# Sliding-window attention and a two-layer MLP on one core: both layers in turn, attention pairs evenly apart, and the third batch loaded ahead of the second weights

## The chip, the core and the metric

The kernel runs on one core of a Trainium2 chip. A core has TensorE (PE in the profile) for matmuls, VectorE (DVE), ScalarE (ACT) and GpSimd (POOL) for element work, and SyncE (SP), which here only issues DMAs. GpSimd and ScalarE can issue DMAs as well. TensorE writes to PSUM, which has eight banks of 128 x 512 float32 values; everything else is in SBUF. The metric is the device time of one execution in microseconds (us): before the change a median of 378.02, from 376.28 to 382.29 in three runs. The execution that the profile shows spans 374.9 us.

## The reference

Attention with a causal window of 64 keys over 8 batches, 8 heads, 576 positions and a head size of 64; then two matrix products with `h - tanh(h)` between them, over 4608 tokens.

```python
# q, k, v: (8, 8, 576, 64)
scores = (1 / np.sqrt(64)) * np.matmul(q, k.transpose(0, 1, 3, 2))
rel = pos[:, None] - pos[None, :]
scores = np.where((rel >= 0) & (rel < 64), scores, -1e9)
attn = np.exp(scores - scores.max(-1, keepdims=True))
attn = attn / (attn.sum(-1, keepdims=True) + 1e-9)
x = np.matmul(attn, v).transpose(0, 2, 1, 3).reshape(4608, 512)
h = x @ w_in                 # (4608, 2048)
out = (h - np.tanh(h)) @ w_out   # (4608, 512), float32
```

## The kernel before

**Attention** is worked by pairs of heads: a batch has four pairs, and pair g belongs to batch g // 4. Each pair goes through these steps. Loads of q and k (`load`, `load_all`) and of v (`load_v`, `load_v_all`) come on GpSimd's DMA queue and turn float32 into bf16. `cast` (L112) brings two heads side by side. `tr` (L259) transposes q and k on TensorE into a PSUM bank, and ScalarE and VectorE copy them to `qT` and `kT`; for batch 7 `bounce` (L124) and `tr_dma` (L136) do it through DRAM with a transposing DMA on SyncE. `scores` (L326) makes nine matmuls in three groups, each followed by an exponential on ScalarE into `PT`. `masking` (L334) multiplies by the window's mask on VectorE. `pv` (L342) makes nine matmuls of `PT` with the value windows `vw` into banks 5 to 7, and `norm` (L349) divides on VectorE into `xs`. Once two pairs or a whole batch are done, x is transposed into a chunk tile `xT`: by `x_tr` (L359) on TensorE or by `x_dma` (L371) on SyncE. Batches 0 and 1 use the variants `tr_heads`, `tr_rows`, `tile_scores` and `tile_pv`, in the same sense.

A **value window** is 128 keys: window j holds block j-1 in partitions 0 to 63 and block j in partitions 64 to 127. `cast_v` (L170) fills `vb` from the loaded v. `windows_v` (L157) then copies a whole window from `vb` by DMA. The other way is `keys_v` (L174), which copies the upper half only, and `shift_v` (L179), which fills the lower halves from the upper ones: on VectorE (`shift_dve`, L465) or by one DMA. There is one `vb`, two `vw` (even and odd batches), one buffer for a loaded v and two each for q and k.

**The MLP** is worked by chunks of 512 tokens, nine in all. A first-layer op h(c, m) is four 128 x 512 matmuls (L403) into a bank, tanh on ScalarE (L408), and a subtraction on VectorE into `gT` (L415), which frees the bank. `hp_bank` names the bank: two in turn, or three in some stretches. A second-layer op y(c, st) is four matmuls (L429) of a quarter of the sum; after four of them ScalarE copies the bank (L434) and SyncE sends 256 KB to the output (L436).

**The order is written by hand.** The program is a row of slots h = 0, 1, 2, ... `OPS` (L438) puts at most one op into a slot, and `items` (filled by `at`, L451) any number of attention steps or loads. The loop at L622 records each slot's op, its items, and then the subtraction of a first-layer op. Every engine works its own instructions in that order, so a slot is a position in each engine's queue and no fixed time. `AHEAD` (L387) says how many second-layer ops of the chunk before run ahead of a chunk's first layer. With a lead of n, a chunk has n second-layer ops in a row, then both layers in turn, then n first-layer ops in a row. `FIRST` (L422) reorders the first eight second-layer ops so that those that need only the first half of `w_out` come first.

`STEPS` (L572) gives for batches 2 to 7 the slot a of each pair: transposes at a and a+2, scores at a+5, a+7, a+9, masking at a+11, `pv` at a+13 to a+15, norm at a+15. `LOADS` gives the slots of the loads of k, q and v, and `VALUES` the first slot and the step of the v casts and the first slot of the windows. `pace` (L460) holds a load on GpSimd until a given first-layer op is done.

Of the kernel before, what the change touches and what calls it, by code (L numbers as in the profile page):

```python
# [15 lines left out]
def kernel(  # L16
# [9 lines left out]
    nc = tc.nc  # L26
    B, H, S, D = q.shape
    NP = H // 2
    NJ = S // 64
# [7 lines left out]
    NC = NT // TOK  # L37
    M = d_ff // 128
# [32 lines left out]
    vw = [const.tile([128, NJ, H, D + 1], BF16, name=f"vw{i}") for i in range(2)]  # L71
# [3 lines left out]
    qT = [const.tile([128, 2, S], BF16, name=f"qt{i}") for i in range(NR)]  # L75
# [6 lines left out]
    def move(eng, o, i):  # L82
        if eng is nc.scalar:
            nc.scalar.activation(o, i, ACT.Copy)  # L84
        else:
            eng.tensor_copy(o, i)  # L86
# [83 lines left out]
    def cast_v(b, pr, eng=nc.gpsimd):  # L170
        move(eng, vb[:, :, 2 * pr:2 * pr + 2, 0:D].rearrange("p e h d -> p h e d"),
             stage.pop((b, pr, "v")).rearrange("p h (e d) -> p h e d", d=D))

    def keys_v(b, j, eng=nc.sync):  # L174

        eng.dma_start(out=vw[b % 2][64:128, j].rearrange("p h c -> p (h c)"),
                      in_=vb[8 * j:8 * j + 8].rearrange("p e h c -> p e (h c)"))
# [15 lines left out]
    def w_in_tile(ki, m):  # L193
        i = m // 8
        f = 512 * (m // 4 % 2) + m % 4
        return w_in_sb[i][:, ki, f:f + 4 * 127 + 1:4]
# [41 lines left out]
    def chunk_tile(c):  # L238
        if c not in xT:
            xT[c] = xt_pool.tile([128, WPC, 2, 128], BF16, tag="xT", name="xT")  # L240
        return xT[c]
# [142 lines left out]
    gT = {}  # L384
    HID = {}

    AHEAD = {1: 8, 2: 8, 3: 6, 4: 4, 5: 4}  # L387

    def hp_bank(c, m):

        m0 = M - AHEAD.get(c, 0)
        if m < m0:
            return m % 2
        a, b = m0 % 2, 1 - m0 % 2
        return {8: (a, b, 2), 6: (a, 2, b), 4: (a, b, 2)}[M - m0][(m - m0) % 3]

    def hp_mm(c, ms, split):

        outs = [ps[:, hp_bank(c, m), :] for m in ms]
        for kis in ((0, 2), (1, 3)) if split else ((0, 1, 2, 3),):  # L400
            for m, hp in zip(ms, outs):
                for ki in kis:
                    nc.tensor.matmul(hp, w_in_tile(ki, m),  # L403
                                     chunk_tile(c)[:, :, ki % 2, 64 * (ki // 2):64 * (ki // 2) + 64],
                                     start=(ki == 0), stop=(ki == 3))
        for m, hp in zip(ms, outs):
            th = sm_pool.tile([128, TOK], F32, tag="th", name="th")
            nc.scalar.activation(th, hp, ACT.Tanh)  # L408
            HID[c, m] = hp, th

    def g_sub(c, m):
        hp, th = HID.pop((c, m))
        if m == 0:
            gT[c] = g_pool.tile([128, M, TOK], BF16, tag="gT", name="gT")
        nc.vector.tensor_tensor(gT[c][:, m, :], hp, th, ALU.subtract)  # L415

    def yp_bank(c, s):
        if c == 0:
            return (2, 1, 2, 2)[s]
        return (0, 2)[s % 2] if c == NC - 1 else 2  # L420

    FIRST = (0, 1, 4, 5, 2, 3, 6, 7)  # L422

    def yp_mm(c, st):
        s, part = divmod(st, 4)
        yp = ps[:, yp_bank(c, s), :]
        for i in range(4):
            m = 4 * part + i
            nc.tensor.matmul(yp, gT[c][:, m, s * 128:(s + 1) * 128], w_out_sb[:, m, :],  # L429
                             start=(m == 0), stop=(m == M - 1))  # L430
# [7 lines left out]
    OPS = {}  # L438
    for m in range(M):
        OPS[2 * m] = "h", 0, m  # L440
        OPS[32 * NC + 2 * m + 1] = "y", NC - 1, m
    for c in range(1, NC):
        n = AHEAD.get(c, 0)
        for m in range(M):
            OPS[32 * c + (n + 2 * m if m < M - n else 16 + m)] = "h", c, m
            st = FIRST[m] if c == 1 and m < 8 else m
            OPS[32 * c + (m if m < n else 2 * m - n + 1)] = "y", c - 1, st

    items = {}

    def at(h, fn, *args):  # L451
        items.setdefault(h, []).append((fn, args))
# [3 lines left out]
    def flush():  # L456
        if done:
            y_out(*done.pop())
# [10 lines left out]
    V, A, G, Y = nc.vector, nc.scalar, nc.gpsimd, nc.sync  # L469
# [63 lines left out]
        cast(g, "k", eng)  # L533
        cast(g, "q", eng)

    at(8, lambda: nc.vector.memset(vw[1][0:64, 0], 0.0))
    at(9, cast_pair, 4, V)
    at(11, cast_pair, 5, V)
    at(12, lambda: [cast_v(1, pr, V) for pr in range(NP)])
    at(13, lambda: [keys_v(1, j, (G, Y)[j % 2]) for j in range(NJ)])  # L540
    at(13, load_w_out, 0)
    at(13, load_w_out, 1)
    at(13, load_v_all, 2)
    for g in 8, 9, 10, 11:
        at(13, load, g, "k", G)
        at(13, load, g, "q", G)
    at(19, cast_pair, 6, V)
    at(22, cast_pair, 7, V)
    for g, t, s0, s1 in (4, 11, 13, 14), (5, 14, 15, 15), (6, 21, 24, 25), (7, 24, 27, 28):
        at(t, tr_rows, g, "k", 2, V)  # L550
        at(t + 1, tr_rows, g, "q", 3, A)
        at(s0, tile_scores, g, 0, (4, 5))
        at(s1, tile_scores, g, 1, (6, 7) if g < 6 else (4, 5))
    at(25, shift_dve, 1, 0, 4)
    for pr in range(NP):
        at(27 + 2 * pr, tile_pv, 4 + pr, (6, 7))
    at(31, x_tr, 1, 0, 0, 4, 3, A)
    at(32, x_tr, 1, 0, 4, 9, 4, A)
    at(36, x_tr, 1, 1, 0, 4, 3, V)
    at(37, x_tr, 1, 1, 4, 9, 4, A)  # L560
    at(33, lambda: nc.vector.memset(qT[1], 0.0))

    at(100, more_zeros, 0)
    at(118, more_zeros, 1)

    def behind_x(b):

        last = ((b + 1) * NJ - 1)
        nc.gpsimd.tensor_copy(tick, chunk_tile(last // WPC)[0:1, last % WPC, 0, 0:1])

    LOADS = {3: (50, 50, 50), 4: (73, 75, 77), 5: (98, 100, 102), 6: (130, 134, 126), 7: (145, 143, 162)}
    STEPS = {2: (39, 44, 49, 54), 3: (63, 73, 79, 84), 4: (93, 102, 108, 114), 5: (121, 127, 133, 138),  # L572
             6: (146, 153, 160, 167), 7: (174, 182, 190, 198)}
    VALUES = {2: (38, 0, 42), 3: (61, 1, 65), 4: (87, 1, 91), 5: (112, 2, 120), 6: (140, 2, 152), 7: (170, 2, 178)}
    at(36, cast_pair, 8, G)
    at(37, cast_pair, 9, G)
    at(40, cast_pair, 10, G)
    at(45, cast_pair, 11, G)
    for g in range(2 * NP, B * NP):
        b, pr = divmod(g, NP)  # L580
        a = STEPS[b][pr]
        cv, cs, ky = VALUES[b]
        at(cv + cs * pr, cast_v, b, pr, V if b == 2 else G)
        if b == 7:
            at(a - 14, cast_q, g)
            at(a - 13, cast, g, "k")
            at(a - 12, bounce, g, "q")
            at(a - 11, bounce, g, "k")
            at(a - 6, tr_dma, g, "q")
            at(a - 5, tr_dma, g, "k")  # L590
        else:
            if b > 2:
                at(a - 7, cast, g, "q")
                at(a - 5, cast, g, "k")
            at(a, tr, g, "q", 3, A, V)
            at(a + 2, tr, g, "k", 3, A)
        for i in range(3):
            at(a + 5 + 2 * i, scores, g, i, 4)
            at(a + 13 + i, pv, g, i)
        at(a + 11, masking, g)  # L600
        at(a + 15, norm, g)
        if b < 5:
            if pr % 2:
                at(a + 16, x_tr, b, pr // 2, 0, 4, 3, V)
                at(a + 17, x_tr, b, pr // 2, 4, 9, 3, A)
        elif pr == NP - 1:
            at(a + 16, x_dma, b)
        if pr == 0:
            for j in range(NJ):
                at(ky + j // 2, windows_v, b, j, Y)  # L610
            if b == 2:
                continue
            hk, hq, hv = LOADS[b]
            for h, f in sorted(((hq, (load_all, b, "q")), (hk, (load_all, b, "k")), (hv, (load_v_all, b))),
                               key=lambda x: x[0]):
                if b > 3:
                    at(h, pace, h)
                if (b, h) == (7, hv):
                    at(h, behind_x, 5)
                at(h, *f)  # L620

    for h in range(32 * NC + 32):  # L622
        op = OPS.get(h)
        if op:
            flush()
        if op and op[0] == "h":
            c, m = op[1:]
            if c == 0 and m == 0:
                hp_mm(c, (0, 1), True)
            elif c > 0 or m > 1:  # L630
                hp_mm(c, (m,), False)
        elif op:
            yp_mm(*op[1:])
            if op[2] % 4 == 3:
                done.append((op[1], op[2] // 4))
        for fn, args in items.pop(h, []):
            fn(*args)
        if op and op[0] == "h":
            g_sub(*op[1:])
# [31 lines left out]
```

The softmax here doesn't subtract the row's maximum and nothing guards it: scores larger than these inputs give would overflow.

## Time and profile before

| What | From the profile before |
|---|---|
| Span of the profiled execution | 374.9 us |
| TensorE, VectorE, ScalarE, GpSimd busy | 327.1, 201.2, 183.9, 104.5 us |
| First-layer matmuls (L403), second-layer (L429) | 150.2, 142.6 us busy |
| One subtraction (L415), one tanh (L408) | 690, 598 ns |
| Half a norm's product (L357), one masking (L336) | 755, 747 ns |
| First-layer ops begin, last tanh begins | 25.6, 356.25 us |
| Halves of `w_out` landed | 52.2, 57.7 us |
| v, k, q of batch 2 landed | 61.4 to 67.7 us |

Busy time of TensorE includes the overlap of matmuls in its pipeline, so the table of lines gives more per matmul than the pace at which they follow each other. The page cuts the span into 40 slices of 9.4 us and gives each engine's busy share in tenths; the clock row is the TensorE clock as a share of full speed. In the waits, a line names who waited, for whom, the total, the number of waits and the longest. In the chain, each piece is the work or the transfer that the next piece waited for.

### The profile page before, as it was taken

What the parts mean: (1) busy time and instruction counts of PE and PEld (TensorE: products, weight loads), DVE (VectorE), ACT (ScalarE), POOL (GpSimd) and SP (SyncE); (2) the same over time, 40 slices, a digit from 0 to 9 for tenths busy, and PEclk for the clock granted to TensorE, in tenths of its full rate; (3) what the DMA queues carried; (4) which work ended last, traced back from release to release, by engine and by line L of the source; (5) the groups of instructions that cost most, each with busy time, mean ns of one, the idle gap of its engine ahead of it and who ended that gap; (6) DMA issues with size and microseconds to landing.
All of it is one profiled execution on the core that took longest, in us unless ns stands there. A gap on an engine that the chain in (4) does not pass through costs nothing.

```text
span 374.9 us, 6143 instructions
## 1 busy us (share of the span) xinstructions
PE 327.1 (87%) x2366; PEld 178.8 (48%) x2398; DVE 201.2 (54%) x332; ACT 183.9 (49%) x338; POOL 104.5 (28%) x153
## 2 busy tenths in 40 slices
PE   7776889988889988999899937797799999999995
PEld 3543454555445544555565513453355544444442
DVE  4557684448556764567668613565466543433400
ACT  3534663766456745667565713554254444444321
POOL 8911804507024616631337325110000000000000
PEclk9989999999999999999999996999699999999999
DMA  8999899792639279345956983448941311001012
GB/s 158 168 174 185 134 200 182 133 221 57 118 69 180 59 120 175 73 78 101 154 93 92 186 149 81 79 104 165 175 96 40 60 60 58 28 28 59 28 57 84
DMA packets 49918, 41.80 MB, mean 111 GB/s; under 512 B 18496, under 2 KB 43584, under 8 KB 49888
## 3 DMA queue, kind: packets, MB, share of 16 engines
q0 software_dynamic: 20816, 18.73, 33.9%
q1 hardware_dynamic: 28720, 22.24, 25.7%
q10 hardware_dynamic: 352, 0.43, 0.4%
q8 instruction: 19, 0.31, 0.3%
q14 instruction: 11, 0.09, 0.1%
HBM read 36.70 MB, written 11.21 MB: 128 GB/s over the span
## 4 chain that ended last, share of the span: by engine, by line
PE 57%; DMA 14%; DVE 12%; ACT 5%; issue 5%; POOL 4%; SPq 2%; ACTq 0%; POOLq 0%; DVEq 0%
PE ps L429 24%; PE ps L403 24%; DMA vall<-in_v_dram 7%; DMA vw<-vb 6%; DVE xs L357 5%; DVE gT L415 3%; PE ps L346 2%; PE ps L330 2%; ACT th L408 2%; PE ps L263 2%; SPq L161 1%; PE ps L363 1%; DVE qt L86 1%; DMA qt<-qd 1%; ACT ysb L434 1%
## 5 line engine op out<-in xcount | busy, mean ns | idle before, releaser
L403 PE MATMUL ps<-xT,wi 128*128 128x512 bf16 x576 | 150.2, 386 | 4.8 <-DVE gT L415 4.1
L429 PE MATMUL ps<-w_out_sb,gT 128*128 128x512 bf16 x545 | 142.6, 383 | 3.8 <-ACT ysb L434 1.3
L415 DVE TENSOR_TENSOR gT<-ps,th 128x512 bf16<-128x512 f32 x144 | 98.6, 690 | 86.3 <-ACT th L408 85.2
L408 ACT ACTIVATE th<-ps 128x512 f32<-128x512 f32 x144 | 86.0, 598 | 89.2 <-PE ps L403 85.6
L403 PEld LDWEIGHTS <-wi 128*128 128x128 bf16 x576 | 61.2, 114 | 53.6 <-issue 11.4
L429 PEld LDWEIGHTS <-gT 128*128 128x128 bf16 x576 | 54.0, 98 | 63.1 <-issue 11.6
L332 ACT ACTIVATE pt<-ps 128x384 bf16<-128x384 f32 x72 | 35.2, 489 | 47.7 <-PE ps L330 47.7
L346 PE MATMUL ps<-vw,pt 128*128 128x130 bf16 x216 | 25.7, 221 | 16.2 <-DMA vw<-vb 13.5
L357 DVE TENSOR_TENSOR xs<-ps,rc 64x576 bf16<-64x576 f32 x48 | 36.2, 755 | 1.1
L434 ACT ACTIVATE ysb<-ps 128x512 f32<-128x512 f32 x36 | 21.4, 595 | 17.3 <-PE ps L429 17.1
L346 PEld LDWEIGHTS <-pt 128*128 128x128 bf16 x216 | 18.2, 98 | 23.8 <-issue 4.2
L86 DVE COPY qt<-ps 64x576 bf16<-64x576 bf16 x20 | 15.2, 759 | 22.5 <-ACT qt L84 22.5
L330 PE MATMUL ps<-qt,kt 128*128 128x128 bf16 x216 | 24.2, 222 | 1.9 <-DMA qt<-qd 1.8
L86 POOL COPY kb<-kall 96x768 bf16<-96x768 bf16 x24 | 19.9, 829 | 17.5 <-DMA kd<-kb 10.1
L86 POOL COPY vb<-vall 72x1024 bf16<-72x1024 bf16 x20 | 20.6, 1052 | 13.8 <-DMA vall<-in_v_dram 13.8
L330 PEld LDWEIGHTS <-kt 128*128 128x128 bf16 x216 | 16.7, 99 | 13.1 <-issue 3.4
L86 POOL COPY qb<-qall 96x768 bf16<-96x768 bf16 x20 | 16.7, 834 | 17.1 <-DMA qall<-in_q_dram 8.6
L353 DVE RECIPROCAL rc<-ps 128x9 f32<-128x9 f32 x24 | 5.2, 218 | 27.0 <-PE ps L346 26.7
L336 DVE TENSOR_TENSOR pt<-pt,ps 128x1152 bf16<-128x1152 bf16 x24 | 17.9, 747 | 1.0 <-ACT pt L332 1.0
L463 POOL COPY tick<-gT 1x1 bf16<-1x1 bf16 x12 | 2.1, 179 | 49.3 <-DVE gT L415 49.3
L84 ACT ACTIVATE xT<-ps 128x512 bf16<-128x512 bf16 (+4 forms) x20 | 8.6, 479 | 14.5 <-PE ps L363 14.5
L84 ACT ACTIVATE kt<-ps 128x576 bf16<-128x576 bf16 x20 | 13.0, 651 | 4.5 <-PE ps L263 4.5
(74 smaller groups left out, 205.8 us busy)
## 6 DMA issues: line engine op xcount, KB each, us to landing
out_dram<-ysb SPq DMA_DIRECT2D x36, 256.0 KB
vw<-vb SPq DMA_DIRECT2D x48, 130.0 KB
vall<-in_v_dram POOLq DMA_DIRECT2D x7, 576.0 KB, 11.5
qall<-in_q_dram POOLq DMA_DIRECT2D x5, 576.0 KB, 6.3
kall<-in_k_dram POOLq DMA_DIRECT2D x5, 576.0 KB, 6.7
wi<-in_moe_w_in_dram POOLq DMA_DIRECT2D x2, 1024.0 KB, 15.1
w_out_sb<-in_moe_w_out_dram POOLq DMA_DIRECT2D x2, 1024.0 KB, 13.9
kall<-in_k_dram POOLq DMA_DIRECT2D x11, 144.0 KB, 15.4
```

What stands on the lines that cost most here:

```text
L84: nc.scalar.activation(o, i, ACT.Copy)
L86: eng.tensor_copy(o, i)
L330: nc.tensor.matmul(sp[:, i, :], kT[g % NR][:, 64 * j:64 * j + 128], qT[g % NR][:, :, 64 * j:64 * j + 64], start=True, stop=True)
L332: nc.scalar.activation(PT[g % NPT][:, 3 * grp:3 * grp + 3, :], sp, ACT.Exp, scale=scale)
L336: nc.vector.tensor_tensor(p, p, mask.unsqueeze(1).to_broadcast([128, 2 * NJ, 64]), ALU.mult)
L346: nc.tensor.matmul(ps[:, 5 + grp, 130 * i:130 * i + 130], PT[g % NPT][:, j, :], vw[b % 2][:, j, 2 * pr:2 * pr + 2, :], start=True, stop=True)
L357: nc.vector.tensor_tensor(xo[r, :, :, pr, :], ov[r, :, :, h, 0:D], rc[r].to_broadcast([64, 3, 3, 64]), ALU.mult)
L403: nc.tensor.matmul(hp, w_in_tile(ki, m), chunk_tile(c)[:, :, ki % 2, 64 * (ki // 2):64 * (ki // 2) + 64], start=(ki == 0), stop=(ki == 3))
L408: nc.scalar.activation(th, hp, ACT.Tanh)
L415: nc.vector.tensor_tensor(gT[c][:, m, :], hp, th, ALU.subtract)
L429: nc.tensor.matmul(yp, gT[c][:, m, s * 128:(s + 1) * 128], w_out_sb[:, m, :], start=(m == 0), stop=(m == M - 1))
L434: nc.scalar.activation(ysb, ps[:, yp_bank(c, s), :], ACT.Copy)
```

## The change

The change rewrites the hand-written order; what is computed stays the same.

- *The MLP's order.* Chunk 0's and chunk 1's first layers come first; second-layer ops of chunk 0 begin at slot 49. From chunk 2 on the two layers take turns throughout, without a lead, eight slots later than before. `FIRST` goes, and the first six ops of chunk 0 use three banks.
- *The start.* v of batch 1 is cast at slot 6 instead of 12. v, k and q of batch 2 are loaded ahead of `w_out`, which moves from slot 13 to 27 behind the windows of batch 2. Casts of batch 2 go from GpSimd to VectorE, and its windows are built by `keys_v` and shifts on VectorE.
- *The pairs* stand 7 to 8 slots apart (before: 5 to 10). Batch 4's x is transposed by DMA instead of TensorE; the x transposes of batches 2 and 3 have slots of their own (`XTR`).
- *The values* of batches 5 to 7 are cast earlier against their use, and their windows are built by `keys_v` and one shift DMA on SyncE. The load of v for batch 7 no longer waits for batch 5's x.

```diff
-    AHEAD = {1: 8, 2: 8, 3: 6, 4: 4, 5: 4}
-
     def hp_bank(c, m):
-
-        m0 = M - AHEAD.get(c, 0)
-        if m < m0:
-            return m % 2
-        a, b = m0 % 2, 1 - m0 % 2
-        return {8: (a, b, 2), 6: (a, 2, b), 4: (a, b, 2)}[M - m0][(m - m0) % 3]
+        return m % 3 if c == 0 and m < 6 else m % 2
...
-            return (2, 1, 2, 2)[s]
+            return 2
...
-    FIRST = (0, 1, 4, 5, 2, 3, 6, 7)
...
-        OPS[32 * NC + 2 * m + 1] = "y", NC - 1, m
-    for c in range(1, NC):
-        n = AHEAD.get(c, 0)
-        for m in range(M):
-            OPS[32 * c + (n + 2 * m if m < M - n else 16 + m)] = "h", c, m
-            st = FIRST[m] if c == 1 and m < 8 else m
-            OPS[32 * c + (m if m < n else 2 * m - n + 1)] = "y", c - 1, st
+        OPS[32 + 2 * m] = "h", 1, m
+        OPS[49 + 2 * m if m < 8 else 56 + m] = "y", 0, m
+        for c in range(2, NC + 1):
+            if c < NC:
+                OPS[32 * c + 8 + 2 * m] = "h", c, m
+            OPS[32 * c + 9 + 2 * m] = "y", c - 1, m
...
-    at(12, lambda: [cast_v(1, pr, V) for pr in range(NP)])
-    at(13, lambda: [keys_v(1, j, (G, Y)[j % 2]) for j in range(NJ)])
-    at(13, load_w_out, 0)
-    at(13, load_w_out, 1)
-    at(13, load_v_all, 2)
+    at(6, lambda: [cast_v(1, pr, V) for pr in range(NP)])
+    at(7, lambda: [keys_v(1, j, (G, Y)[j % 2]) for j in range(NJ)])
+    at(7, load_v_all, 2)
     for g in 8, 9, 10, 11:
-        at(13, load, g, "k", G)
-        at(13, load, g, "q", G)
+        at(7, load, g, "k", G)
+        at(7, load, g, "q", G)
...
+    at(26, lambda: [cast_v(2, pr, V) for pr in range(NP)])
...
+    at(27, lambda: [keys_v(2, j, G) for j in range(NJ)])
+    at(27, load_w_out, 0)
+    at(27, load_w_out, 1)
+    at(27, load_all, 3, "q")
+    at(27, load_all, 3, "k")
+    at(27, load_v_all, 3)
+    at(41, shift_dve, 2, 0)
+    at(42, shift_dve, 2, 4)
...
-    LOADS = {3: (50, 50, 50), 4: (73, 75, 77), 5: (98, 100, 102), 6: (130, 134, 126), 7: (145, 143, 162)}
-    STEPS = {2: (39, 44, 49, 54), 3: (63, 73, 79, 84), 4: (93, 102, 108, 114), 5: (121, 127, 133, 138),
-             6: (146, 153, 160, 167), 7: (174, 182, 190, 198)}
-    VALUES = {2: (38, 0, 42), 3: (61, 1, 65), 4: (87, 1, 91), 5: (112, 2, 120), 6: (140, 2, 152), 7: (170, 2, 178)}
+    LOADS = {4: (74, 75, 77), 5: (101, 104, 97), 6: (132, 136, 119), 7: (156, 160, 150)}
+    STEPS = {2: (30, 38, 46, 54), 3: (63, 70, 77, 84), 4: (91, 98, 105, 112), 5: (119, 126, 134, 142)}
+    XTR = {9: (58, 60), 11: (70, 71), 13: (88, 90), 15: (100, 102)}
+    VALUES = {3: (64, 1, 68), 4: (84, 1, 90), 5: (107, 2, 115), 6: (124, 5, 142), 7: (156, 5, 174)}
...
-        a = STEPS[b][pr]
+        a = STEPS[b][pr] if b in STEPS else 8 * g - 44
...
-        if b < 5:
-            if pr % 2:
-                at(a + 16, x_tr, b, pr // 2, 0, 4, 3, V)
-                at(a + 17, x_tr, b, pr // 2, 4, 9, 3, A)
-        elif pr == NP - 1:
+        if g in XTR:
+            at(XTR[g][0], x_tr, b, pr // 2, 0, 4, 3, V)
+            at(XTR[g][1], x_tr, b, pr // 2, 4, 9, 3, A)
+        if b > 3 and pr == NP - 1:
             at(a + 16, x_dma, b)
...
-                at(ky + j // 2, windows_v, b, j, Y)
+                at(ky + j // 2, windows_v if b < 5 else keys_v, b, j, Y)
+            if b > 4:
+                at(ky + 7, shift_v, b, 0, NJ - 1)
...
-                if (b, h) == (7, hv):
-                    at(h, behind_x, 5)
```

More of the change, by code (lines that the diff above doesn't have):

```diff
@@ L534, in cast_pair @@
         cast(g, "q", eng)
-    at(8, lambda: nc.vector.memset(vw[1][0:64, 0], 0.0))
+    at(3, lambda: nc.vector.memset(vw[1][0:64, 0], 0.0))
+    at(6, lambda: [cast_v(1, pr, V) for pr in range(NP)])
+    at(7, lambda: [keys_v(1, j, (G, Y)[j % 2]) for j in range(NJ)])
+    at(7, load_v_all, 2)
+    for g in 8, 9, 10, 11:
+        at(7, load, g, "k", G)
+        at(7, load, g, "q", G)
     at(9, cast_pair, 4, V)
     at(11, cast_pair, 5, V)
-    at(12, lambda: [cast_v(1, pr, V) for pr in range(NP)])
@@ L540 @@
-    at(13, lambda: [keys_v(1, j, (G, Y)[j % 2]) for j in range(NJ)])
-    at(13, load_w_out, 0)
-    at(13, load_w_out, 1)
-    at(13, load_v_all, 2)
-    for g in 8, 9, 10, 11:
-        at(13, load, g, "k", G)
-        at(13, load, g, "q", G)
[L547 to L553, printed above, removed]
@@ L554 @@
-    at(25, shift_dve, 1, 0, 4)
-    for pr in range(NP):
[L556 to L561, printed above, removed]
+    at(18, cast_pair, 6, V)
+    at(20, cast_pair, 7, V)
+    at(22, shift_dve, 1, 0, 4)
+    for g, t, ka, qa, a, b in ((4, (11, 12, 13, 14), 6, 7, (4, 5), (6, 7)), (5, (14, 15, 15, 15), 2, 3, (4, 5), (6, 7)),
+                             (6, (19, 20, 21, 22), 2, 3, (4, 5), (4, 5)), (7, (21, 22, 24, 25), 2, 3, (4, 5), (4, 5))):
+        at(t[0], tr_rows, g, "k", ka, V)
+        at(t[1], tr_rows, g, "q", qa, A)
+        at(t[2], tile_scores, g, 0, a)
+        at(t[3], tile_scores, g, 1, b)
@@ new lines @@
+    for pr in range(NP):
+        at(24 + 2 * pr, tile_pv, 4 + pr, (6, 7))
+    at(26, lambda: [cast_v(2, pr, V) for pr in range(NP)])
+    at(27, lambda: nc.vector.memset(qT[1], 0.0))
+    at(29, x_tr, 1, 0, 0, 4, 3, A)
+    at(30, x_tr, 1, 0, 4, 9, 4, A)
+    at(31, x_tr, 1, 1, 0, 4, 3, V)
+    at(31, x_tr, 1, 1, 4, 9, 4, A)
+    at(27, lambda: [keys_v(2, j, G) for j in range(NJ)])
[3 more added lines that the diff above has]
+    at(27, load_all, 3, "k")
@@ L563 @@
+    at(27, load_v_all, 3)
+    at(41, shift_dve, 2, 0)
+    at(42, shift_dve, 2, 4)
     at(100, more_zeros, 0)
-    at(118, more_zeros, 1)
+    at(116, more_zeros, 1)
     def behind_x(b):
@@ L569, in behind_x @@
         nc.gpsimd.tensor_copy(tick, chunk_tile(last // WPC)[0:1, last % WPC, 0, 0:1])
-    LOADS = {3: (50, 50, 50), 4: (73, 75, 77), 5: (98, 100, 102), 6: (130, 134, 126), 7: (145, 143, 162)}
-    STEPS = {2: (39, 44, 49, 54), 3: (63, 73, 79, 84), 4: (93, 102, 108, 114), 5: (121, 127, 133, 138),
-             6: (146, 153, 160, 167), 7: (174, 182, 190, 198)}
-    VALUES = {2: (38, 0, 42), 3: (61, 1, 65), 4: (87, 1, 91), 5: (112, 2, 120), 6: (140, 2, 152), 7: (170, 2, 178)}
[L575 to L578, printed above, removed]
+    LOADS = {4: (74, 75, 77), 5: (101, 104, 97), 6: (132, 136, 119), 7: (156, 160, 150)}
+    STEPS = {2: (30, 38, 46, 54), 3: (63, 70, 77, 84), 4: (91, 98, 105, 112), 5: (119, 126, 134, 142)}
+    XTR = {9: (58, 60), 11: (70, 71), 13: (88, 90), 15: (100, 102)}
+    VALUES = {3: (64, 1, 68), 4: (84, 1, 90), 5: (107, 2, 115), 6: (124, 5, 142), 7: (156, 5, 174)}
     for g in range(2 * NP, B * NP):
         b, pr = divmod(g, NP)
-        a = STEPS[b][pr]
-        cv, cs, ky = VALUES[b]
-        at(cv + cs * pr, cast_v, b, pr, V if b == 2 else G)
-        if b == 7:
+        a = STEPS[b][pr] if b in STEPS else 8 * g - 44
+        if b == 2:
+            at((28, 33, 41, 49)[pr], cast_pair, g, V)
+        elif b == 7:
             at(a - 14, cast_q, g)
@@ L591 @@
         else:
[L592 to L596, printed above, removed]
+            at(a - 7, cast, g, "q")
+            at(a - 5, cast, g, "k")
+        if b < 7:
+            at(a, tr, g, "q", 2 if g < 10 else 3, A, V)
+            at(a + 2, tr, g, "k", 2 if g < 10 else 3, A)
         for i in range(3):
@@ L601 @@
         at(a + 15, norm, g)
-        if b < 5:
-            if pr % 2:
-                at(a + 16, x_tr, b, pr // 2, 0, 4, 3, V)
-                at(a + 17, x_tr, b, pr // 2, 4, 9, 3, A)
-        elif pr == NP - 1:
+        if g in XTR:
+            at(XTR[g][0], x_tr, b, pr // 2, 0, 4, 3, V)
+            at(XTR[g][1], x_tr, b, pr // 2, 4, 9, 3, A)
+        if b > 3 and pr == NP - 1:
             at(a + 16, x_dma, b)
-        if pr == 0:
+        if b > 2:
+            cv, cs, ky = VALUES[b]
+            at(cv + cs * pr, cast_v, b, pr)
+        if pr == 0 and b > 2:
             for j in range(NJ):
-                at(ky + j // 2, windows_v, b, j, Y)
-            if b == 2:
+                at(ky + j // 2, windows_v if b < 5 else keys_v, b, j, Y)
+            if b > 4:
+                at(ky + 7, shift_v, b, 0, NJ - 1)
+            if b == 3:
                 continue
@@ L615 @@
                                key=lambda x: x[0]):
-                if b > 3:
-                    at(h, pace, h)
-                if (b, h) == (7, hv):
-                    at(h, behind_x, 5)
+                at(h, pace, h)
                 at(h, *f)
-    for h in range(32 * NC + 32):
+    for h in range(32 * NC + 48):
         op = OPS.get(h)
@@ L628 @@
             if c == 0 and m == 0:
-                hp_mm(c, (0, 1), True)
-            elif c > 0 or m > 1:
+                hp_mm(c, (0, 1, 2), True)
+            elif c > 0 or m > 2:
                 hp_mm(c, (m,), False)
```

## The prediction

> **What bounds the kernel now.** I read the page's slices and its clock row first, then the waits of TensorE, the table of stages, the chain, and last the queues of SyncE and GpSimd around the worst gap.
>
> ```profile
> span 374.9 us, 6143 instructions
> ...
> PE 327.1 (87%) x2366; PEld 178.8 (48%) x2398; DVE 201.2 (54%) x332; ACT 183.9 (49%) x338; POOL 104.5 (28%) x153
> ...
> PEclk9989999999999999999999996999699999999999
> ...
> DMA  8999899792639279345956983448941311001012
> ```
>
> TensorE is busy nearly everywhere. The last third is nearly full, two slices near 60% of the span are not, and in those two the clock falls. DMA is full only for the first 80 us.
>
> ```profile
> PE ps L346 <- DMA vw<-vb: 13.5, 9, 6.9
> PE ps L363 <- DVE xs L357: 4.6, 6, 1.0
> PE ps L403 <- DVE gT L415: 4.1, 6, 1.2
> PE ps L346 <- DVE pt L336: 2.6, 3, 1.2
> ```
>
> These are the four largest waits of TensorE (total us, times, longest). The value windows vw, copied by DMA out of vb, lead by far. The next three are TensorE waiting for VectorE.
>
> ```profile
> 155.00:205.00 50.00, 46.75 (x365) 27.64 (x370) 34.76 (x56) 32.13 (x61) 22.90 (x32) 1.00 0.56 94
> ...
> 217.00:240.00 23.00, 12.79 (x81) 6.84 (x82) 7.48 (x12) 6.05 (x11) 8.24 (x11) 0.85 0.54 101
> ...
> 256.00:270.00 14.00, 10.03 (x45) 4.70 (x44) 6.18 (x10) 4.67 (x10) 0.00 (x0) 0.76 0.90 162
> ...
> 298.00:356.00 58.00, 57.74 (x264) 28.37 (x269) 23.51 (x34) 24.62 (x42) 0.00 (x0) 1.00 0.15 49
> ```
>
> Columns: stretch, length, busy PE, PEld, DVE, ACT, POOL, clock, DMA. From 217 to 240 TensorE does 12.79 us of work in 23 us, at clock 0.85. From 298 it loses nothing.
>
> ```profile
> 215.75 1.19 SPq L161
> 217.70 9.61 DMA vw<-vb
> 227.61 1.71 PE ps L429 x4
> ...
> 260.77 4.55 DMA vw<-vb
> ```
>
> This is the chain. A window of batch 6 is issued at 217.7 and lands 9.6 us later; the four matmuls after it take 1.71 us where four take 0.86 elsewhere. The same comes back for batch 7 at 261. The cause is in the queues: SyncE issues x transposes at 210.25 for 2.88 us with the last windows behind them, GpSimd starts the 576 KB load of v for batch 7 at 217.0 (landed about 228.5), and bounces to DRAM go out at 218.6 and 219.5.
>
> **What the Trainium skill says.** (1) "TensorE: Matmul & The Clock Gate", section "What's actually happening": after an idle window of about 3.4 us the array runs at half clock. The trace agrees: 1.71 against 0.86 us after a wait of 6.9 us. So a long wait costs its length and about 2 us more. (2) "DMA: Bandwidth & Descriptors", "Queues, rings and completion order": each DMA engine goes round-robin over its queue rows by packets. So windows share with a load of v that runs beside them; 9.6 us for 130 KB agrees. (3) Same page, "Anatomy of one DMA": a wait for a semaphore is held by the issuing sequencer. That matters for the new shift copy, since everything on SyncE stands behind it.
>
> **The change, part by part.** I count in slots. The change adds eight empty slots ahead of chunk 2, so later a slot s+8 of after holds the matmuls of slot s of before. Prices: an op (four 512-wide matmuls) 0.864 us, from the stall-free pace 1.73 per two ops after 296 us. A pair's attention is six groups of three matmuls at 0.17 and two transposes at 0.25, 1.5 us on TensorE; without transposes 1.0.
>
> *A. Start, up to 48 ops done (layers 1 of chunks 0 and 1, layer 2 of chunk 0), batch 2 through, first pair of batch 3 scored.* In before that state is reached at 107.0 less the eight second-layer ops of chunk 1 already done (6.9), so 100.1. For after I add by stretches.
> Slots 0 to 31: TensorE needs 16 x 0.864 + about 9.4 for batch 1 = 23.2 us, but VectorE needs more: 16 subtractions at 0.68 (10.9), two batches of v casts at 1.42 (2.8), ten k/q casts at 0.35 (3.5), four kT copies at 0.75 (3.0), two shifts (1.4), two memsets (1.0), four norms at 1.04 (4.2), a qT and an xT copy (1.2): 28.0. It starts at 28.35 as in before; with 3 us idle (it idled about 10 in 27 to 60) slot 32 comes at 59.5. The three PSUM banks for the first six ops shorten the first waits (a two-bank pair now takes 2.44 us), and the earlier v casts sit right after v's landing at 29.6.
> Slots 32 to 48: nine first-layer ops with no second-layer op between. TensorE 7.8 + 2.8 attention = 10.6; VectorE nine subtractions 6.2, three qT copies 2.3, masking 0.75, norm 1.7, casts 1.4, two shifts 1.5 = 13.8. VectorE sets the pace; with 0.9 idle, slot 49 comes at 74.2.
> Is w_out there? The queue moves 3.87 MB from 43.9 to 67.7, 163 GB/s. With k and q of batch 1 landed at 40.2 and v windows by 43.5, v and k, q of batch 2 (1.77 MB) take 11 us, to about 54. GpSimd then makes nine window copies at 0.57 behind the v casts (about 52 to 58) and starts w_out: halves at about 64 and 70. First use is at 74, the second half's at 77. So the delay is hidden behind the first layers. The dropped order FIRST, which used half one first, is not needed then.
> Slots 49 to 71: 23 ops (19.9) + 5.8 attention + 2.0 of waits (x transposes one slot after the norm, one y bank in the run of eight) = 27.7: 101.9. **A: +1.8** (from -3 to +9).
>
> *B. From there to all first layers of chunks 0 to 4 and all second layers of chunks 0 to 3.* Before: 100.1 to 215.0 = 114.9 us. After: 96 ops 83.0, 13.9 pairs 21.3, two x transposes by TensorE 1.0 = 105.3. Waits: before, the last eight first-layer ops of a chunk in a row overload VectorE (138.48 and 100.46 wait over 1 us for masking), eight second-layer ops in a row stop on the one y bank (0.2 to 0.5 each), and x transposes stand one slot behind the norm (0.84 four times). With alternation no run of either kind is left, and per 7.5 slots VectorE needs 5.8 and ScalarE 5.5 of about 8 us, so neither binds. Batch 4's x goes by DMA at slot 128, eight slots before chunk 4 reads it: two transposes of about 2.9 us issue together against about 8.5 us. In before's alternating slots 132 to 156 there still was a loss of 2.8 us per 24 slots, in 192 to 216 0.7. I take 6.5 for the 96: 111.8. **B: -3.1** (from -8 to 0).
>
> *C. The rest to the end of the first layers.* Before 215.0 to 356.9 = 141.9. After: 128 ops 110.6 and attention 7 = 117.5, plus waits. Batch 6: v is loaded at slot 119, cast at 124 to 139, windows at 142 to 146, shift at 149, used at 161: 12 slots, some 13 us, before x transposes join the queue at 158. Batch 7: v at 150, no longer held behind batch 5's x; k and q at 156 and 160; bounces from 168. So the v load does not meet the windows or the bounces. But at 174 to 181 SyncE has nine copies at 0.63, two transposes (1.2 to 2.4 each), two bounces, 9.7 us in 5.5 us of slots, and then the shift, which waits for the copies and holds the next transposes. No row of before shows a shift by DMA. The skill's fit in "Anatomy of one DMA", 2.0 + bytes/436e3, gives 3.2 us for 532 KB as an estimate; from above it is the 9.6 us of the congested window. I take 5. It then lands at about 238 of my time scale; first use at slot 193, about 240. Tight; I allow 4 us (1 to 14). **C: 121.5, -20.4.**
>
> *Tail.* Sixteen second-layer ops and the last output, 18 us, unchanged. The casts that go from GpSimd to VectorE are in A; pace copies 0.18 each on GpSimd, which has idle time around them.
>
> Sum: +1.8 - 3.1 - 20.4 = -21.7; 378.0 - 21.7 = **356.3**.
>
> **Rivals.** *Better spacing (about 349):* A breaks even and B loses as little as 192 to 216, -7. For it: its masking and norm waits vanish. Against: those slots had no transposes. *The window wait comes back on SyncE (about 367):* the shift takes the upper price and the following transposes come late, with the clock falling: C +10. For it: SyncE's count above. Against: 12 slots of lead. *Slower (about 387):* the start turns on DMA. If v of batch 2 lands late, its cast on VectorE at slot 26 stops all subtractions behind it, so the h banks and TensorE, and nine copies and w_out stand behind it on GpSimd: up to 13 us, and if batch 7 stalls too (+18 against my C), 356 + 31. For it: DMA is full until 80 us. Against: 163 GB/s puts v at 47 against about 51. *No change (about 375):* half of each.
>
> **How the numbers follow.** Forecast 0.58, better 0.15, window wait 0.12, no change 0.08, slower 0.07. 2% is 370.5 to 385.6. Faster: 0.58 + 0.15 and most of 0.12, less a margin, 0.82; same 0.11; slower 0.07. The range 346 to 372 takes in the first three with the bounds of A and the shift and leaves out about 0.18.
>
> **What would show it.** A: first second-layer op at about 74 with no wait for w_out; VectorE nearly full from 30 to 74. B: no wait of masking over 1 us, fewer for x. C: the window wait falls from 13.5 to under 4 us, clock 1.0 throughout, last first-layer op at about 335. I am wrong if TensorE waits at slots 26 to 32 or 49 to 53 for a load, or if SyncE's shift is the releaser of a value matmul.

## The result, and the profile after

After takes 365.50 us (median of four runs, 364.47 to 365.87), before 377.15 us (four runs). The ratio is 0.971, with a 95% interval from 0.965 to 0.978: faster by about 3%. The forecast was 356.3 us; the time lies in its range, but the gain is little more than half of the forecast one.

The page of after: span, and the slices of TensorE, of its clock and of DMA.

```profile
span 362.8 us, 6139 instructions
...
PE   7777785799879997999999999797999999999995
...
PEclk9989998889999999999999999999899999999999
DMA  9999995993059938946796779458930410011012
```

The two weak places of before near 60% of the span are gone; what is left of them are two slices with a 7. New is a weak stretch at the start, slices 7 to 9 (54 to 81 us), with a clock digit of 8.

TensorE's waits in after, the largest and those that answer to before's (total us, times, longest):

```profile
PE ps L363 <- DVE xs L357: 3.3, 2, 2.3
PE ps L302 <- ACT qs L84: 3.1, 5, 0.7
PE ps L420 <- ACT ysb L425: 2.8, 5, 1.3
...
PE ps L263 <- POOL kb L86: 2.5, 1, 2.5
...
PE ps L330 <- DMA kt<-kd: 1.8, 1, 1.8
...
PE ps L346 <- DVE pt L336: 1.6, 2, 1.1
...
PE ps L346 <- DMA vw<-vw: 0.8, 1, 0.8
```

The wait for the windows out of vb, 13.5 us in before, is gone, and 0.8 us for the shift is left. A wait for a k cast on GpSimd and one for kT are new.

Stages of after (stretch, length, busy PE, PEld, DVE, ACT, POOL, clock, DMA):

```profile
226.00:232.00 6.00, 3.52 (x24) 1.74 (x23) 3.06 (x5) 2.90 (x6) 4.75 (x7) 1.00 0.35 100
232.00:248.00 16.00, 16.00 (x102) 8.79 (x101) 9.81 (x16) 8.92 (x16) 4.82 (x9) 1.00 0.65 137
248.00:258.00 10.00, 7.35 (x40) 3.77 (x38) 3.77 (x7) 2.77 (x5) 0.00 (x0) 0.83 0.95 208
```

Between 226 and 232, and between 248 and 258, TensorE is still idle, for 2.5 and 2.65 us (length less busy time); between them it is full. The chain of after shows who held it:

```profile
203.61 7.75 issue
...
217.50 9.74 issue
...
227.25 0.22 POOL qz L122
...
229.21 0.78 POOL kb L86
...
248.04 0.77 SPq L139
...
248.85 2.99 DMA kt<-kd
```

The two "issue" pieces are GpSimd standing idle: 7.75 us before a cast of v, and 9.74 us before its copy into qz. The waits of GpSimd say for what:

```profile
POOL qz L122 <- DMA qall<-in_q_dram: 9.8, 1, 9.8
POOL vb L86 <- DMA vall<-in_v_dram: 7.8, 1, 7.8
```

GpSimd stood for v of batch 7 until 211.4; the loads of k and q of batch 7, behind that cast in its queue, went out at 212.5 and 214.9. The load of q landed at 227.2, 12.3 us after its issue. Beside it ran the load of k, the x transposes of batch 5 (issued at 211.93 for 4.55 us) and two outputs of 256 KB. The k cast of pair 27 stood behind the copy into qz in GpSimd's queue, and pair 28's bounces, the windows and the shift came late on SyncE.

In the prediction's three sums:

| Part | Before | Forecast for after | After |
|---|---|---|---|
| A: start, to 48 ops done | 100.1 | 101.9 | 109.0 |
| B: to 144 ops done | 114.9 | 111.8 | 111.3 |
| C: to the end of the first layers | 141.9 | 121.5 | 124.6 |
| Tail | 18.0 | 18.0 | 17.9 |

The ends come from the starts of tanh: less 0.86 for its op, chunk 2 begins at about 109, chunk 5 at 220.3; the last tanh starts at 344.34. B is right; A missed by 7 and C by 3.

### The profile page after: what moved, and what is told of

It is laid out like the page before. It is cut to its first block, busy times and chain, and to the rows that moved or that the text cites. A ratio compares the mean times of both kernels' runs of the same rounds, so it can differ in the third digit from the quotient of the medians.

```text
span 362.8 us, 6139 instructions
## 1 busy us (share of the span) xinstructions
PE 325.8 (90%) x2380; PEld 178.5 (49%) x2380; DVE 202.8 (56%) x340; ACT 184.4 (51%) x336; POOL 103.8 (29%) x153
## 4 chain that ended last, share of the span: by engine, by line
PE 66%; DVE 11%; issue 7%; ACT 6%; DMA 5%; POOL 4%; SPq 0%; POOLq 0%; DVEq 0%; ACTq 0%
PE ps L420 29%; PE ps L396 26%; DVE xs L357 3%; PE ps L346 3%; DVE gT L408 2%; DMA w_out_sb<-in_moe_w_out_dram 2%; PE ps L330 2%; DVE qt L86 2%; DMA vall<-in_v_dram 2%; ACT th L401 1%; PE ps L263 1%; ACT qt L84 1%; PE ps L363 1%; DVE vb L86 1%; POOL vb L86 1%
## 5 line engine op out<-in xcount | busy, mean ns | idle before, releaser
L420 PE MATMUL ps<-w_out_sb,gT 128*128 128x512 bf16 x576 | 145.8, 381 | 2.9 <-ACT ysb L425 2.8
L86 DVE COPY qt<-ps 64x576 bf16<-64x576 bf16 x20 | 15.2, 760 | 21.7 <-ACT qt L84 21.7
L346 PE MATMUL ps<-vw,pt 128*128 128x130 bf16 x216 | 24.9, 227 | 2.4 <-DVE pt L336 1.6
L86 POOL COPY qb<-qall 96x768 bf16<-96x768 bf16 x16 | 13.2, 828 | 28.0 <-DVE gT L408 14.4
L336 DVE TENSOR_TENSOR pt<-pt,ps 128x1152 bf16<-128x1152 bf16 x24 | 17.9, 745 | 0.1
L86 POOL COPY kb<-kall 96x768 bf16<-96x768 bf16 x20 | 16.6, 831 | 2.0 <-DMA kall<-in_k_dram 2.0
L176 POOL DMA_DIRECT2D vw<-vb x19 | 11.4, 615 | 9.6 <-DVE gT L408 5.6
L263 PE MATMUL ps<-ident,kb 96*128 96x96 bf16 x120 | 8.6, 209 | 4.8 <-POOL kb L86 2.5
## 6 DMA issues: line engine op xcount, KB each, us to landing
w_out_sb<-in_moe_w_out_dram POOLq DMA_DIRECT2D x2, 1024.0 KB, 12.4
```

The costliest lines, as they stand in the source:

```text
L336: nc.vector.tensor_tensor(p, p, mask.unsqueeze(1).to_broadcast([128, 2 * NJ, 64]), ALU.mult)
L346: nc.tensor.matmul(ps[:, 5 + grp, 130 * i:130 * i + 130], PT[g % NPT][:, j, :], vw[b % 2][:, j, 2 * pr:2 * pr + 2, :], start=True, stop=True)
```

## The experiments

Theory 1: the gain comes from the earlier values of batches 5 to 7, and the new order of the MLP gives nothing or costs. The rival: even spacing and alternation made the room. Each run was timed beside before on the same chip; before's median was 378.1 beside the first four, 379.2 beside the next four, 378.4 beside the last. After itself was timed earlier, beside a before of 377.15, so a difference of a microsecond or two between a run and after is not one to rely on. In the edits, "..." marks what is left out.

**1. The earlier values, in before.** Windows of batches 5 to 7 are built by `keys_v` and one shift, as in after. The loads move too: those of k and q of batch 7 come later than in before (slots 149 and 153, not 145 and 143).

```diff
-    LOADS = {..., 5: (98, 100, 102), 6: (130, 134, 126), 7: (145, 143, 162)}
-    VALUES = {..., 5: (112, 2, 120), 6: (140, 2, 152), 7: (170, 2, 178)}
+    LOADS = {..., 5: (97, 100, 93), 6: (130, 134, 112), 7: (149, 153, 143)}
+    VALUES = {..., 5: (101, 2, 109), 6: (117, 5, 135), 7: (149, 5, 167)}
-                at(ky + j // 2, windows_v, b, j, Y)
+                at(ky + j // 2, windows_v if b < 5 else keys_v, b, j, Y)
+            if b > 4:
+                at(ky + 7, shift_v, b, 0, NJ - 1)
...
-                if (b, h) == (7, hv):
-                    at(h, behind_x, 5)
```

> Theory 1 (the time comes from the earlier values of batches 5 to 7 alone, and the new order of the MLP gives nothing or costs): before with only these values earlier gains at least as much as the whole change, 356 to 366 us, and the wait of the value matmuls on vw falls from 13.5 us to under 5. Rival (the even spacing and the alternation made room for the windows; earlier loads alone only collide elsewhere): 370 to 378 us, with the wait moved to another transfer.

Measured: 362.73 us, ratio 0.962 (0.955 to 0.969). So this part, with before's whole MLP order and spacing, gains all that the change gains. TensorE's waits there, the two that count:

```profile
PE ps L363 <- DVE xs L357: 4.6, 6, 1.0
...
PE ps L346 <- DMA vw<-vb: 0.8, 1, 0.8
```

The window wait is down from 13.5 to 0.8 us with the pairs 5 to 10 slots apart as before; the waits for x are unchanged at 4.6. Theory 1 holds for the change as it is. The edit moves the values earlier and also changes how their windows are built (a half copy and a shift for a whole copy); no run parts the two. In before's trace batches 4 and 5 have whole windows 15 and 14 slots ahead of their use and TensorE waits for none of them, while in batches 6 and 7, with 7 and 9 slots, it waits 8.6 and 3.5 us. That speaks for the lead, though batch 3's whole windows don't fit: 1.4 us of waits in before with 11 slots, none in after with 8.

**2. The earlier values undone in after.**

```diff
-    LOADS = {..., 6: (132, 136, 119), 7: (156, 160, 150)}
-    VALUES = {..., 6: (124, 5, 142), 7: (156, 5, 174)}
+    LOADS = {..., 6: (132, 136, 128), 7: (156, 160, 168)}
+    VALUES = {..., 6: (142, 2, 154), 7: (176, 2, 184)}
```

Windows of batches 6 and 7 are whole ones again, and v of batch 7 waits for batch 5's x. The loads of k and q of batch 7 stay where the change put them.

> After, with the values of batches 6 and 7 loaded, cast and copied as far ahead of their use as in before. Theory 1: the window wait and the slow clock come back, about +12 us, 375 to 380 us. Rival (spacing removed it): within 3 us of after, 364 to 368 us.

Measured: 384.76 us, ratio to before 1.018 (1.010 to 1.026). The waits of TensorE and the chain:

```profile
PE ps L346 <- DMA vw<-vb: 15.2, 7, 7.3
```

```profile
212.56 7.80 DMA vw<-vb
...
222.28 5.84 DMA vw<-vb
```

The wait comes back at its old size though the pairs are evenly apart. The loss is 19 us against after, more than the 12 expected; with the late values the new kernel is slower than before by 1.8%. Not all of that need be the order of the MLP: run 5 finds 6 us in the loads of k and q of batch 7, which are not undone here.

**3. The weights ahead of batch 2 again, in after.**

```diff
+    at(7, load_w_out, 0)
+    at(7, load_w_out, 1)
     at(7, load_v_all, 2)
...
-    at(27, load_w_out, 0)
-    at(27, load_w_out, 1)
```

> After, with w_out loaded ahead of v, q and k of batch 2 again. If the order of the loads matters because v of batch 2 is cast at slot 26 on VectorE in front of the subtractions, v lands about 11 us later, that cast stops VectorE for about 8 us, and the time rises by 6 to 10 us, 371 to 376. If instead the late w_out is what makes the start slow, the time falls by 2 to 5 us, 360 to 363. If neither is on the path, no change within 1 us.

Measured: 371.81 us, ratio 0.984 (0.979 to 0.990), 6.3 us above after's median. VectorE at slot 26:

```profile
53.46 0.82 DVE L324 TENSOR_TENSOR xs<-ps,rc 128x640 bf16<-128x640 f32 x1
59.28 1.45 DVE L86 COPY vb<-vall 72x1024 bf16<-72x1024 bf16 x4 [5.00 <-DMA vall<-in_v_dram]
60.66 0.68 DVE L408 TENSOR_TENSOR gT<-ps,th 128x512 bf16<-128x512 f32 x1
```

VectorE stands 5.0 us for v of batch 2, with the subtraction behind the cast; TensorE waits 6.2 us for that subtraction. So within the new order the load of batch 2 must be first. In after itself w_out lands at 71.3 and 76.3, and its first use is at 78.8: hidden, as forecast.

**4. Three banks for the first eight ops of chunk 1.**

```diff
-        return m % 3 if c == 0 and m < 6 else m % 2
+        return m % 3 if c == 0 and m < 6 or c == 1 and m < 8 else m % 2
```

The transposes of pair 9 go to bank 3.

> After, with three banks in turn for the first eight first-layer ops of chunk 1, and the transposes of the second pair of batch 2 in bank 3. If VectorE's amount of work sets the pace of slots 32 to 48 (13.8 us of work against 10.6 on TensorE), no change, within 1 us. If the round trip of a bank through ScalarE and VectorE sets it, 2 to 3 us less, 362 to 363.5 us.

Measured: 364.93 us, ratio 0.968 (0.961 to 0.975): no change that can be told from after. In its trace slots 32 to 48 take 12.5 us from tanh to tanh, in after's 15.2; but the clock differs there. The stretch in this run, and then in after (the third number from the end is the clock):

```profile
62.00:78.00 16.00, 12.45 (x99) 7.13 (x100) 12.99 (x22) 10.44 (x20) 3.56 (x5) 1.00 1.04 182
```

```profile
62.00:78.00 16.00, 13.53 (x85) 7.58 (x84) 10.65 (x19) 9.49 (x19) 2.98 (x4) 0.80 1.06 184
```

At a clock of 0.89 in this stretch the slots took 14.1 us with three banks (run 7) and 14.4 and 14.2 with two (runs 5 and 6). At full clock they took 12.5 with three (runs 4 and 9) and 13.3 with two (run 3, whose start differs). So the banks are worth at most about 0.9 of the 2.7 us, and the clock is most of it. VectorE does not set a pace of 13.8 us either, since 12.5 was reached.

**5. q and k of batch 7 earlier,** and its v two slots later.

```diff
-    LOADS = {..., 7: (156, 160, 150)}
+    LOADS = {..., 7: (146, 140, 152)}
```

> After, with q, k and v of batch 7 loaded at slots 140, 146 and 152 in place of 160, 156 and 150. Theory: in after the cast of q of batch 7 waits on GpSimd for a load of q that runs beside the x transposes of batch 5 (12.3 us to landing), the k cast of pair 27 stands behind it, and SyncE's bounces, windows and shift all start late; earlier loads take away TensorE's 2.5 us wait for the k cast, the 1.8 and 0.8 us waits for kT and the shift and the half clock after them, 5 to 7 us in all: 358 to 361. Rival (SyncE's own list of copies at slots 174 to 181 is the bound): only the 2.5 us go, and the later waits grow; 363 to 365.

Measured: 359.37 us, ratio 0.950 (0.940 to 0.959), 6.1 us less than after. Slots 168 to 200 take 33.2 us in its trace against 39.45 in after's, and the waits for the k cast and the shift are gone. The waits for kT are still 1.8 us in sum, in two places (246.4 and 255.4). The theory's price was right in total. So the place of these loads on GpSimd is worth more than C's excess of 3.1 us over its forecast. Which of their neighbours made q's load slow (k's load, the x transposes, the outputs) this run does not tell apart. With these loads early the new order is level with run 1 (0.962) or ahead of it; the two intervals overlap.

**6. A second bank for chunk 0's second layer.**

```diff
         if c == 0:
-            return 2
+            return (2, 2, 0, 2)[s]
```

> After, with the third group of chunk 0's second layer in bank 0 in place of bank 2, so that the run of eight second-layer ops does not stop for the copy of its bank. If these waits (1.3 and 0.5 us) are on the path: 1 to 2 us less, 363.5 to 364.5. If TensorE then only arrives earlier at the x transposes of pairs 10 and 11, which wait for VectorE: no change.

Measured: 365.01 us, ratio 0.964 (0.957 to 0.972): no difference from after. Slots 48 to 72 take 30.3 us in its trace against 32.4, so the waits for the bank did go. In this execution they were given back at the x transposes of pair 15:

```profile
144.09 0.40 PE L363 MATMUL ps<-ident,xs 128*128 128x128 bf16 x4 [2.28 <-DVE xs L357]
145.33 1.91 PE L420 MATMUL ps<-w_out_sb,gT 128*128 128x512 bf16 x4
```

After the same 2.3 us wait the clock fell to half in this trace and in those of runs 2, 4 and 8; in after's and those of runs 3 and 5 it stayed full. Here that took 1.7 us.

**7. All mended: 4, 5 and 6, and the x transposes of pair 15 at slots 102 and 103 instead of 100 and 102.** Only the last edit is shown.

```diff
-    XTR = {..., 15: (100, 102)}
+    XTR = {..., 15: (102, 103)}
```

> After, with the three banks in chunk 1, the earlier loads of batch 7, the second bank for chunk 0's second layer, and the x transposes of pair 15 two slots later. If the causes add up (2.9 us seen in the start of the run with three banks, 5 to 7, 1 to 2, and 1.5 of the 2.3 us wait for x): 353 to 357. If one wait takes the place of the other: 358 to 362.

Measured: 356.75 us, ratio 0.941 (0.931 to 0.952). Slots 72 to 104 take 37.4 us in its trace against 39.6. The wait at the x transposes of pair 15 was from VectorE: in after its norm stands behind a copy of qT that waits 2.2 us for ScalarE. Two waits on DMA were left after 200 us:

```profile
PE ps L330 <- DMA kt<-kd: 2.1, 2, 1.3
PE ps L346 <- DMA vw<-vw: 2.1, 1, 2.1
```

The first is for kT of batch 7, in two pieces at 245.6 and 254.6. The second is for the shift of batch 6, not of batch 7: it ends at 209.7, and the chain of this run has that shift as

```profile
200.03 9.59 DMA vw<-vw
```

The load of v of batch 7 ran beside it, from 198.4 to 210.1. Half clock follows this wait: four matmuls take 1.71 us at 211.8.

**8. Chunk 0's second layer early.** Its ops stand in slots 33 to 63, w_out is loaded first, and batch 2 is cast and worked some nine slots later, as in before.

```diff
-        OPS[49 + 2 * m if m < 8 else 56 + m] = "y", 0, m
+        OPS[33 + 2 * m] = "y", 0, m
...
-    STEPS = {2: (30, 38, 46, 54), ...}
+    STEPS = {2: (39, 44, 49, 54), ...}
```

> After, with chunk 0's second-layer ops spread over slots 33 to 63, w_out loaded first again, and batch 2 cast, copied and worked some nine slots later as in before. Theory (the start is slower than before because two first layers, which need VectorE, stand back to back with no second-layer op to fill TensorE): chunk 2 begins at about 100 to 104 us of the trace in place of 109, and the time is 357 to 362. Rival (VectorE has the same work in either order and TensorE waits elsewhere): chunk 2 begins at 107 or later, 364 to 368.

Measured: 366.76 us, ratio 0.969 (0.962 to 0.976): the rival's number. But its reason was not VectorE's load, which is 6.85 us of the 14.5 from 95 to 109.5. All 48 ops are done soon after the last tanh of chunk 1, which begins at 94.8; then chunk 2 waits for the x of batch 2, and begins at about 109 as in after, in part at half clock (0.68 from 95 to 109.5). The chain of this run there:

```profile
97.13 0.76 DVE qt L86
...
97.92 0.23 DVE rc L353
...
98.18 0.75 DVE xs L357
98.94 0.76 DVE xs L357
99.72 0.77 DVE pt L336
...
100.53 0.83 PE ps L346 x6
```

Transposes, exponentials, masks and norms of the last pairs follow one another with no MLP op between them.

**9. The values of batch 7 earlier as well**, on top of run 7. The expectation takes run 7's shift wait for one of batch 7.

```diff
-    LOADS = {..., 7: (146, 140, 152)}
-    VALUES = {..., 7: (156, 5, 174)}
+    LOADS = {..., 7: (148, 140, 143)}
+    VALUES = {..., 7: (152, 4, 166)}
```

> The mended kernel (three banks in chunk 1, a second bank for chunk 0's second layer, pair 15's x later, q and k of batch 7 early), with the values of batch 7 earlier as well: loaded at slot 143, cast at 152 to 164, windows at 166, shift at 173. In the mended kernel TensorE still waits 2.1 us for the shift and 2.1 us for kT behind it on SyncE. If the shift's place in SyncE's queue is the cause, both go and the time falls by 3 to 5 us, to about 352 to 354. If the DMA engines are simply full there, it stays at 356 to 357.

Measured: 353.82 us, ratio to before 0.935 (0.928 to 0.942). From 200 to 260 us TensorE's waits are these two alone:

```profile
PE ps L346 <- DVE pt L336: 0.5, 1, 0.5
PE ps L420 <- ACT ysb L425: 0.2, 1, 0.2
```

Both waits went, and by two ways. The shift of batch 7 was issued at 225.1 (run 7: 239.3), and the transposes of kT behind it on SyncE came earlier with it: there its place in the queue was the cause. Batch 6's shift was issued at 204.0, when the load of v of batch 7, moved nine slots earlier, had landed (203.5). Earlier in the trace, at 177 us, a wait of 1.2 us for batch 5's shift is new. The gain over run 7 is 2.9 us between medians from two chips, and their intervals overlap (run 7: 0.931 to 0.952). This version beats before by 24.6 us and after by 11.7 us (in medians). Run 1, with before's order, was not given the like of these mends, so how much of this needs the new order is open.

## Why the prediction was right, and where it was off

The two stalls for the windows were found and their end was priced about right; in run 1's trace, with before's order, part C takes 124 us, as it does in after. What went wrong is mostly A.

*A was mis-sized.* The forecast was +1.8 us, the trace has +8.9. Three of its terms were too small. Slots 0 to 31 ended at about 61.3 and not 59.5: VectorE was to be idle for 3 us, and it was busy for 25.8 of 33.0, with 5.6 us of waits for tanh. Slots 32 to 48 took 16.5 and not 14.7; the step said that VectorE's 13.8 us of work set the pace. That doesn't hold: VectorE is busy for 10.45 us of these 16.5, run 4 reached 12.5 from tanh to tanh, and the clock, for which A had no term, explains most of the difference. The stretches of after, 28.3 to 61.3 and 61.3 to 77.8, have VectorE as their third busy time:

```profile
28.30:61.30 33.00, 23.71 (x297) 13.72 (x295) 25.84 (x52) 19.06 (x34) 16.45 (x26) 1.00 0.94 142
61.30:77.80 16.50, 14.19 (x86) 7.87 (x87) 10.45 (x19) 9.29 (x18) 3.67 (x5) 0.79 1.03 180
```

Slots 49 to 71 took 31.2 and not 27.7: 1.85 us for the y bank where I put 2.0 for everything, and 2.9 more for x and qT copies that stand in line on VectorE.

Behind the terms lies what I had not seen. Chunk 2 can begin only when batch 2's x is there, and it begins at about 107 us in before and 109 in after and in run 8. Before fills that time with eight second-layer ops of chunk 1, since its lead lets them run; after has only those of chunk 0 left. By chunk 2's first op before has done 56 ops and after 48. Taking the eight ops off before's time, as I did, supposes that after's attention and copies fit into the shorter time too. In run 8 they do not: its 48 ops are done early, and TensorE then waits 7.4 us in five pieces between 95 and 109.5. In after itself the waits from slot 49 on are 4.8 us in all, so eight more ops could have filled no more than that. This is read from the traces; no run put the lead into after, so what the lead is worth stays open.

*w_out is hidden*: right, though its halves land 6 to 7 us later than forecast; the second has 2.5 us to spare at the second layer's first op instead of 4. *The early load of batch 2 is needed at slot 26*: right, by run 3, and that was the rival's fear.

*B* was right: -3.6 us against -3.1. Before's wait for masking in this part, 1.2 us at 138, is gone, and one of 0.5 is the longest left (one of 1.1 at 72 is new, in A). The waits for x became one: pair 15's grew to 2.3 us, where the forecast had them all go. It counted 0.84 four times; before's six are 0.84 three times, 1.01, 0.75 and 0.34.

*C* had the right mechanism and a size off by 3. The window wait went from 13.5 to 0.8 us for the shift, against "under 4". The 4 us that I allowed for SyncE's queue turned out as 2.5 us for the k cast, 1.8 for kT, 0.8 for the shift and the half clock after it. Of these the forecast named only the queue of SyncE. The first cause was GpSimd: it stands for v of batch 7, q's load goes out behind that and takes 12.3 us to landing, and the k cast of the pair before waits behind it (run 5: 6.1 us). "The v load does not meet the windows or the bounces" was right; that GpSimd's own queue would hold the loads of k and q, and that these would meet other transfers, was missed. Of the signs, the shift as releaser of a value matmul did appear, with 0.8 us; the clock was not 1.0 throughout, VectorE was busy for 32.8 of the 44 us from 30 to 74 and not nearly full, and the last first-layer op came at 344 and not 335.

Of what the prediction took from the skill, two things can be checked. A wait is held by the issuing sequencer ("DMA: Bandwidth & Descriptors", "Anatomy of one DMA"): run 9 agrees, where the transposes of kT come earlier with the shift in front of them and 2.1 us of waits go. The fit in that section is stated for DMAs that GpSimd issues, and the shift goes out from SyncE: batch 7's took 4.4 us in after, near the 5 that I took, and batch 6's 9.6 us in run 7. The half clock after a wait ("TensorE: Matmul & The Clock Gate", "What's actually happening") came at 252 us in after, 1.71 us for four matmuls, and in runs 2, 4, 6 and 8 after only 2.3 us of waiting, less than the 3.4 us that the page states.

## What to carry to other kernels

When a transfer is late, ask first how many slots of work lie between its issue and its use, and move it alone before rewriting the order: the slots of the loads, casts and copies of three batches, with windows built by half copies and a shift, gave all of this change's gain. In-order queues pass a late load on: look at what stands behind the instruction that waits (a k cast behind q's copy, a transpose behind a shift). And before taking a lead away, look for the wait that its work fills; that is read from the traces here, not tried.

## What the runs showed of the hardware

The same wait of TensorE for pair 15's x, 2.28 or 2.29 us, stands in seven traces. In four of them (runs 2, 4, 6 and 8) half clock followed, with 1.90 or 1.91 us in the records for the next four second-layer matmuls; in three (after, runs 3 and 5) the clock stayed full, with 1.03. A 576 KB load took 6.7 us in before (179.8 to 186.5, with v's load beside it for the first 3.8), 12.3 us in after beside k's load, DMA transposes and outputs, and 12.4 us in run 9 (k of batch 7, from 195.3) beside v's load, window copies and a shift, with no transposes issued. A shift of 520 KB by DMA took 4.4 us in after (245.4 to the matmul that waited for it at 249.8), and 9.6 in run 7 beside a load of v.
